# Loading batch 0's input in 96-row and 7-row pieces, and issuing the first tables and the mixing weights after the ninth unit's write

## The chip, the cores and the metric

One core of a Trainium2 chip runs the whole program. The metric is the device time of one execution in microseconds. An execution's span is the time from its first to its last instruction in the profile; the device time is a little more.

## What is computed

The reference has two parts: a spectral mixing layer over 8 sequences of 2496 rows of 256 numbers, and a mixture of experts over the 19968 rows that come out.

```python
X = np.fft.rfft(x, axis=1)                       # x: 8 x 2496 x 256
Yr = Xr @ w_r - Xi @ w_i + b_r
Yi = Xr @ w_i + Xi @ w_r + b_i
Yr = np.sign(Yr) * np.maximum(np.abs(Yr) - lam, 0.0)      # Yi the same
y = np.fft.irfft(Y, n=x.shape[1], axis=1)
...
logits = x @ w_gate                              # x: y as 19968 x 256
# greedy: pairs (row, expert) by falling logit, 2496 rows for each of 8 experts
h = np.maximum(x[mask] @ w1[e], 0.0)
out[mask] = h @ w2[e]
```

## The kernel before, in words

The Fourier transform of 2496 = 39 x 64 points goes in stages. For each batch, **stage 1** multiplies by a table that holds three copies of the 39-point transform side by side. Its input tile has 117 rows: 39 row positions for each of three column groups j, which start 22 columns apart. One of 11 units is two columns: one matmul with 512 free elements, a copy out of PSUM, and a write to the scratch tensor T (called T1 in the code, L1102). **Stage 2** reads T back, transposed by the way it is laid out, into the tile sh (six reads in batch 0, L1108), and multiplies by the 64-point table FG (L1121). ACT and DVE split each result into a high and a low part (xTh, xTl, L1130 to L1133). **Stage 3** multiplies by the mixing weights wt (L1140), DVE adds the bias (L1146), ACT and DVE apply the threshold (L1147, L1148). Stages 4 and 5 are the inverse transform (L1156, L1187). Stages 2 to 4 go in ten pairs p of table columns, two to a pair. The router and the experts follow in one program.

The order of the work is set by a planner (class Plan). Each piece of work is a task with an engine, an estimated duration, a position number and its dependences; the planner simulates the engines and emits, on each engine, the ready task that can start first, ties by position. So another estimate or dependence early in the program changes the fixed order in which each engine's queue is filled. Input loads of batch 0 have positions from -90 upwards.

What matters for the change:

- Batch 0's input is loaded by SP at L1060: for each chunk of 2 or 4 columns three loads of 39 rows, one for each j, 18 loads in all. The first chunk goes to a tile xt, the others into the tile that later is sh.
- Stage 1 of batch 0 is L1084; the units' results go round the tiles s1st, s4st, yst and s2c (L1099 on DVE, L1097 on ACT).
- Loads of constants are issued on POOL. Chunk 0 of the table cF (columns 0 to 4) waits for unit 0's copy through a one-element copy on POOL, a "gate" (L978); chunk 1 (columns 4 to 10) waits for unit 6's copy; the mixing weights w_r and w_i (L1015), the biases (L1010) and w_gate (L1019) wait for unit 10's copy (L1008). The rest (cG, cD, cF's chunks 2 and 3) waits for the first result of stage 2.
- L997 to L1000 turn FG's columns, in groups of four, into the inverse table; a group needs its chunk of cF. After stage 1, TensorE runs 40 matmuls on zeros (L1093, L1094).
- SP's loads and stores and ACT's load share eight completion semaphores, so the k-th of them waits until the (k-8)-th has landed.

Of the kernel before, what the change touches and what calls it, by code (L numbers as in the profile page):

```python
# [19 lines left out]
N1, N2 = 39, 64  # L20
B, S, D, E, F_ = 8, 2496, 256, 8, 1024
# [50 lines left out]
def const_arrays():  # L72
    D1, Fm, G, D5 = dft_consts()
    two = lambda m: np.ascontiguousarray(np.stack(split(m)))
    return dict(cD1=np.concatenate([two(D1), D1.astype(np.float32)[None]]), cF=Fm.astype(np.float32), cG=two(G[:, 0]), cD5=two(D5))
# [841 lines left out]
WU = 10  # L917
# [3 lines left out]
def phase_a(K, H, x, w_r, w_i, b_r, b_i, w_gate, cD1, cF, cG, cD5, YD, LG, NB=B):  # L921

    nc, plan = K.nc, K.plan
# [117 lines left out]
    def batch(b):  # L1041
# [6 lines left out]
        for c, (g0, n) in enumerate(CH):  # L1048
# [4 lines left out]
            xt.append(t)  # L1053
            for j in range(3):
# [6 lines left out]
                add_dma(pos1(g0 / 2) - 1.5 if b else -90 + c, em, 39 * m * 1024, [], [x0, t] if c and not b else [t], after=last_sh)  # L1061
        T1, sh, ev = K.dram("T1", [128, 20, 256]), sb("sh", [128, 20, 256]), []
        for u in range(NU):
# [5 lines left out]
            k_, M, gs_, n = *((117, 120) if u < 10 else (78, 80)), slice(0, 2), 512  # L1069
# [33 lines left out]
            if not b and u == 10: last_sh.append(d)  # L1103
        shq = []
# [394 lines left out]
```

## Time and profile before

| | |
|---|---|
| median of 3 runs | 1552.83 us (1551.01 to 1554.67) |
| the profiled execution's own time | 1552.06 us |
| its span | 1549.9 us |
| TensorE (PE) busy | 1516.3 us, 98% of the span |
| VectorE (DVE) / ScalarE (ACT) / GpSimd (POOL) busy | 1071.6 / 856.3 / 669.1 us |
| mean granted TensorE clock | 0.994 |
| moved by DMA | 208.23 MB |

The profile's page gives shares of the whole span. The view by stretch gives, for a piece of the span, each engine's busy time with the number of instructions, the granted TensorE clock as a share of full speed, the mean busy share of the 16 DMA engines and what they moved. The chain of waits follows the work that ended last backwards, step by step. The timeline lists instructions in order of time, with the idle time ahead of one and what ended it. q1 is the queue of SP's transfers, q0 that of POOL's.

### The profile page before, as it was taken

What the parts mean: (1) busy time and instruction counts of PE and PEld (TensorE: products, weight loads), DVE (VectorE), ACT (ScalarE), POOL (GpSimd) and SP (SyncE); (2) the same over time, 40 slices, a digit from 0 to 9 for tenths busy, and PEclk for the clock granted to TensorE, in tenths of its full rate; (3) what the DMA queues carried; (4) which work ended last, traced back from release to release, by engine and by line L of the source; (5) the groups of instructions that cost most, each with busy time, mean ns of one, the idle gap of its engine ahead of it and who ended that gap; (6) DMA issues with size and microseconds to landing.
All of it is one profiled execution on the core that took longest, in us unless ns stands there. A gap on an engine that the chain in (4) does not pass through costs nothing.

```text
span 1549.9 us, 31539 instructions
## 1 busy us (share of the span) xinstructions
PE 1516.3 (98%) x10927; PEld 1357.0 (88%) x10927; DVE 1071.6 (69%) x3524; ACT 856.3 (55%) x1870; POOL 669.1 (43%) x891
## 2 busy tenths in 40 slices
PE   7999999999899999999999999999999999999998
PEld 5999999999778877888788989889989889989998
DVE  3676767677975684889889889897777765552321
ACT  2768888787678887544535334344343443553332
POOL 2246566564545445343334434434335343343332
PEclk9999999999999999999999999999999999999999
DMA  9678777877668567433213122121211212311110
GB/s 272 192 245 258 220 250 217 249 233 243 217 179 262 178 192 214 143 129 129 86 45 100 47 69 69 50 93 54 70 59 59 89 57 69 114 56 45 43 48 29
DMA packets 144199, 208.23 MB, mean 134 GB/s; under 512 B 28751, under 2 KB 108575, under 8 KB 144030
## 3 DMA queue, kind: packets, MB, share of 16 engines
q1 hardware_dynamic: 127244, 162.30, 33.8%
q0 software_dynamic: 16656, 43.77, 9.0%
q8 instruction: 88, 1.44, 0.4%
q14 instruction: 81, 0.66, 0.1%
q10 hardware_dynamic: 130, 0.06, 0.0%
HBM read 121.31 MB, written 84.75 MB: 133 GB/s over the span
## 4 chain that ended last, share of the span: by engine, by line
PE 81%; DVE 6%; issue 4%; ACT 3%; DMA 3%; POOL 1%; SPq 0%; POOLq 0%; DVEq 0%; ACTq 0%
PE ps L665 25%; PE ps L639 19%; PE ps L1140 11%; PE p L639 6%; PE ps L1121 4%; PE ps L1156 3%; PE p L1077 2%; PE p L1187 2%; PE ps L624 2%; PE both L1210 2%; PE p L1191 1%; ACT ajunk L510 1%; PE ps L658 1%; PE ps L1228 1%; DVE junk L423 1%
## 5 line engine op out<-in xcount | busy, mean ns | idle before, releaser
L1140 PE MATMUL ps<-wt,xTh 128*128 128x256 f32 x1280 | 243.4, 288 | 2.2 <-DVE y L1148 1.1
L1140 PEld LDWEIGHTS ps<-wt,xTh 128*128 128x128 f32 x1280 | 198.6, 189 | 10.5 <-issue 5.8
L1140 PE MATMUL ps<-wt,xTl 128*128 128x256 f32 x640 | 178.8, 279 | 0.0
L678 POOL DMA_INDIRECT out_dram<-xTh,li x64 | 67.1, 1048 | 249.4 <-ACT xTh L674 212.7
L423 DVE SCALAR_TENSOR_TENSOR junk<-h_m,st,h_AG 128x156 bf16<-128x156 f32 (+1 forms) x472 | 161.2, 387 | 2.6
L956 POOL TENSOR_TENSOR zl<-y,zh 128x512 fp32r<-128x512 f32 x80 | 106.4, 1330 | 119.3 <-ACT zh L953 115.4
L1217 POOL TENSOR_TENSOR yTl<-yr,yTh 128x468 bf16<-128x468 f32 (+1 forms) x88 | 96.9, 1103 | 118.4 <-ACT yTh L1216 109.6
L1140 PEld LDWEIGHTS ps<-wt,xTl 128*128 128x128 f32 x640 | 120.4, 188 | 0.2 <-DVE xTl L1133 0.2
L1121 PE MATMUL ps<-FG,sh 128*128 128x128 f32 x640 | 97.9, 281 | 5.0 <-DMA sh<-T 4.6
L678 POOL DMA_INDIRECT out_dram<-xTl,li x64 | 65.7, 1026 | 85.5 <-ACT xTl L674 68.9
L665 PE MATMUL ps<-FG,yTh 128*128 128x256 f32 x441 | 102.1, 282 | 0.0
L1121 PEld LDWEIGHTS ps<-FG,sh 128*128 128x128 f32 x640 | 87.3, 194 | 13.6 <-DMA sh<-T 5.0
L674 ACT COPY xTl<-ps 128x256 f32<-128x256 f32 x80 | 29.9, 373 | 124.2 <-PE ps L665 100.2
L956 POOL TENSOR_TENSOR s2l<-s2c,s2h 120x512 fp32r<-120x512 f32 (+2 forms) x60 | 77.2, 1291 | 42.5 <-DVE s2h L953 31.0
L674 ACT COPY xTh<-ps 128x256 f32<-128x256 f32 x72 | 26.9, 374 | 110.2 <-PE ps L665 93.0
L665 PE MATMUL ps<-FG,y 128*128 128x256 f32 x414 | 86.8, 281 | 0.0
L956 DVE TENSOR_TENSOR xl<-xt,xh 117x512 fp32r<-117x512 f32 (+1 forms) x66 | 65.4, 992 | 25.1 <-ACT xh L953 23.8
L1131 DVE TENSOR_TENSOR xTl<-ps,xTh 128x512 fp32r<-128x512 f32 x80 | 54.8, 686 | 39.9 <-ACT xTh L1130 39.6
L665 PEld LDWEIGHTS ps<-FG,yTh 128*128 128x128 f32 x441 | 74.3, 188 | 0.9
L1215 DVE TENSOR_TENSOR yr<-both,yTh 128x468 f32<-128x468 f32 (+1 forms) x77 | 48.2, 625 | 35.5 <-ACT yTh L1214 32.7
L1148 DVE SCALAR_TENSOR_TENSOR y<-ps,y 128x512 f32<-128x512 f32 x80 | 55.1, 688 | 21.9 <-ACT y L1147 20.4
L665 PE MATMUL ps<-FG,s1st 128*128 128x256 f32 x329 | 69.5, 285 | 0.0
(755 smaller groups left out, 5094.6 us busy)
## 6 DMA issues: line engine op xcount, KB each, us to landing
xt<-in_moe_w_dram SPq DMA_DIRECT2D x64, 512.0 KB
T<-s4st SPq DMA_DIRECT2D x80, 256.0 KB
sh<-T SPq DMA_DIRECT2D x39, 512.0 KB
s2c<-T SPq DMA_DIRECT2D x80, 240.0 KB
YD<-yst SPq DMA_DIRECT2D x80, 234.0 KB
T<-s1st SPq DMA_DIRECT2D x73, 240.0 KB
xt<-in_x_dram SPq DMA_DIRECT2D x105, 156.0 KB
sh<-in_x_dram SPq DMA_DIRECT2D x14, 156.0 KB
```

The costliest lines, as they stand in the source:

```text
L423: v(cols + 59 + 1400 * K.extra, p, lambda k=k: V.scalar_tensor_tensor(junk[k % 2].t[:, 0:cols], H.m[:, 0:cols], c.t[:, k // ng:k // ng + 1 ...
L639: T.matmul(ps.t[:, 0:w], lhsT=W1.t[:, a, m, 128 * ft:128 * ft + 128], rhs=x_.t[:, 0:w], start=q + m == 0, stop=q + m == 3)
L665: T.matmul(ps.t[0:M], lhsT=a.t[:, 128 * q:128 * q + M], rhs=W2.t[:, w_, ft], start=k == 0, stop=k == 23)
L674: else: plan.add('A', .27, pos + 1, lambda: A.copy(o.t[0:M], ps.t[0:M]), [ps], [o])
L678: ins = P.indirect_dma_start(out=self.out, out_offset=bass.IndirectOffsetOnAxis(ap=oi.t[0:M, oo + t:oo + t + 1], axis=0), in_=o.t[0:M], in ...
L956: lambda: eng.tensor_tensor(lb[1](), src(), hb[1](), op=OP.subtract), [srcb, hb[0]], [lb[0]])
L1121: T.matmul(ps.t[:, i, 128 * dt:128 * dt + 128], lhsT=sh.t[:, k, 128 * dt:128 * dt + 128], rhs=Ft.t[:, k], start=True, stop=True)
L1131: plan.add('V', dve(512), pos, lambda th=th, tl=tl, src=src, apart=apart: apart(V.tensor_tensor(cols(tl, 64, 192), src(), cols(th, 64, 192 ...
L1140: T.matmul(ps3.t[:, i], lhsT=a.t[:, i, dt, o:o + 128], rhs=wt[c].t[:, w, dt], start=n == 0, stop=n == 11)
L1148: plan.add('V', dve(512), pos + 1.282, lambda y=y, ps3=ps3, t=t: V.scalar_tensor_tensor(y.t, ps3.t, 0.0, t.t, op0=OP.max, op1=OP.subtract) ...
L1215: plan.add('V', dve(2 * W), pos + 0.376, lambda yh=yh, yr=yr, psT=psT, W=W: V.tensor_tensor(yr.t[:, :, 0:W], psT.t[:, :, 0:W], yh.t[:, 0, ...
L1217: yq.append(plan.add('P', pool(2 * W), pos + 0.376, lambda yh=yh, yl=yl, yr=yr, W=W: P.tensor_tensor(yl.t[:, :, 0:W], yr.t[:, :, 0:W], yh. ...
```

## The change

- Batch 0's input tile gets another row order: rows 0 to 95 hold row position n = 0 to 31 with its three j side by side (row 3n + j), rows 96 to 116 hold the seven positions 32 to 38 for each j. The stage-1 table is stored with the same order of rows (`first`).
- For each chunk SP issues one load of 96 rows. For the first chunk it also issues three loads of 7 rows. For the other chunks POOL issues the 7-row loads as seven larger ones that span two or three chunks. SP's 18 loads become 9, and POOL gets 7.
- The three gates of chunk 0, chunk 1 and the weights are replaced by one: a one-element memset on POOL into the tile of the ninth unit (u = 8, tile s1st), which has to wait until that unit's write to T has landed. Chunk 0, then w_r and w_i, the biases, chunk 1 and w_gate are issued behind it.
- The last unit's matmul takes 117 rows where it took 78.

```diff
+    first = np.array([39 * j + n for n in range(NM) for j in range(3)] + [39 * j + n for j in range(3) for n in range(NM, N1)])
+    return dict(cD1=np.concatenate([two(D1), D1[first].astype(np.float32)[None]]), ...
...
-            g = gate((at(0), at(6), at(0, 0), at(0, 0))[q])
-            add_dma(-50 + q if q > 1 else -99 + q, lambda k0=k0, k1=k1: P.dma_start(Ft.t[:, k0:k1], cF[:, k0:k1, :]), 65e3 * (k1 - k0), [], [Ft, BF_[q]], 'P', after=g)
+            g = gate(at(0, 0)) if q > 1 else gates['w8']
+            add_dma(-50 + q if q > 1 else (-99, -96.5)[q], lambda k0=k0, k1=k1: P.dma_start(Ft.t[:, k0:k1], cF[:, k0:k1, :]), 65e3 * (k1 - k0), [], [Ft, BF_[q]], 'P', after=g)
...
     def load_weights(after):
-        b = gates['s1st', 0, WU]
-        first = [plan.add('P', 0.15, -99, lambda: P.tensor_copy(spacer[0:1, 0:1], b.t[0:1, 0, 0:1]), [b])]
+        b, d = gates['wr']
+        first = gates['w8'] = [plan.add('P', 0.15, -99.5, lambda: P.memset(b.t[0:1, 0, 0:1], 0.0), [], [], after=[d], uses=[b])]
...
+            if not b:
+
+                def rows(p, r0, nr, src0, ap, g0=g0, n=n, t=t):
+                    return lambda: nc.sync.dma_start(t.t[r0:r0 + nr, 0:n, :], bass.AP(tensor=x.tensor, offset=x.offset + (src0 + g0) * D, ap=ap + [[1, n * D]]))
+                add_dma(-90 + c, rows(0, 0, 3 * NM, 0, [[64 * D, NM], [22 * D, 3]]), 3 * NM * n * 1024, [], [x0, t] if c else [t])
+                if not c:
+                    for j in range(3): add_dma(-90 + c, rows(0, 3 * NM + 7 * j, 7, 64 * NM + 22 * j, [[64 * D, 7]]), 7 * n * 1024, [], [t])
+                continue
...
+        if not b:
+            for c0, c1 in ((1, 3), (3, 6)):
+                g0, g1 = CH[c0][0], sum(CH[c1 - 1])
+                for j in range(3):
+                    for a, z, jj in ((g0, min(g1, 20 if j == 2 else g1), j), (20, g1, 1)) if j == 2 and g1 > 20 else ((g0, g1, j),):
+                        def late(j=j, a=a, z=z, jj=jj):
+                            P.dma_start(x0.t[3 * NM + 7 * j:3 * NM + 7 * j + 7, a - 2:z - 2], bass.AP(tensor=x.tensor, offset=x.offset + (64 * NM + 22 * jj + a) * D, ap=[[64 * D, 7], [1, (z - a) * D]]))
+                        add_dma(-95 + c0, late, 7 * (z - a) * 1024, [], [x0] + xt[c0:c1], 'P')
...
-            k_, M, gs_, n = *((117, 120) if u < 10 else (78, 80)), slice(0, 2), 512
+            k_, M, gs_, n = *((117, 120) if u < 10 else (78 if b else 117, 80)), slice(0, 2), 512
...
+            if not b and u == 8: gates['wr'] = (st, d)
```

What is left out places the lines above in their functions and sets NM = 32.

**POOL, from its first work of the program on.** Before (spacer copies are the gates):

```order
masks.py:199 AFFINE_SELECT h_idn<-h_idn 128x128
L978 COPY spacer<-s1st_232 1x1
L981 DMA FG_238<-cF 128x512
L978 COPY spacer<-yst_274 1x1
L981 DMA FG_238<-cF 128x768
L1008 COPY spacer<-yst_338 1x1
L1015 DMA y_343<-in_w_r_dram 128x2x256
L1015 DMA y_345<-in_w_i_dram 128x2x256
L1010 DMA bt<-in_b_r_dram 64x256
L1019 DMA y_357<-in_moe_w_gate_dram 128x2x8
L1010 DMA bt<-in_b_i_dram 64x256
```

With the change (the memset of s1st is the new gate):

```order
L1078 DMA sh_165<-in_x_dram 7x2048 x3
L1078 DMA sh_165<-in_x_dram 7x3072 x2
L1078 DMA sh_165<-in_x_dram 7x2560
L1078 DMA sh_165<-in_x_dram 7x512
masks.py:197 MEMSET h_idn 128x128
masks.py:199 ISA
masks.py:199 AFFINE_SELECT h_idn<-h_idn 128x128
L1010 MEMSET s1st_282 1x1
L983 DMA FG_336<-cF 128x512
L1017 DMA y_338<-in_w_r_dram 128x2x256
L1017 DMA y_343<-in_w_i_dram 128x2x256
L1012 DMA bt<-in_b_r_dram 64x256
```

Seven loads of input rows now come first on POOL, chunk 0 of cF moved from the first gate to the same gate as the weights, and chunk 1 and the second bias went further back.

**DVE, from the first mixing weight split to the second bias addition.** Here xTl is the low part of stage 2's result for pairs 0, 1 and 2, y the result of the threshold, xl the low part of batch 1's input, bt the bias. Before:

```order
L1131 TENSOR_TENSOR xTl_401<-ps_384,xTh_395 128x4x128
L1133 TENSOR_TENSOR xTl_401<-xTh_395,ps_384 128x4x64
L1012 TENSOR_SCALAR bt<-bt 128x256
L1131 TENSOR_TENSOR xTl_428<-ps_392,xTh_404 128x4x128
L1133 TENSOR_TENSOR xTl_428<-xTh_404,ps_392 128x4x64
L1146 TENSOR_TENSOR ps_415<-ps_415,bt 128x512
L1148 SCALAR_TENSOR_TENSOR y_467<-ps_415,y_465 128x512
L1131 TENSOR_TENSOR xTl_487<-ps_447,xTh_483 128x4x128
L1133 TENSOR_TENSOR xTl_487<-xTh_483,ps_447 128x4x64
L1146 TENSOR_TENSOR ps_452<-ps_452,bt 128x512
```

With the change, from pair 2 on:

```order
L1150 TENSOR_TENSOR xTl_474<-ps_454,xTh_463 128x4x128
L1152 TENSOR_TENSOR xTl_474<-xTh_463,ps_454 128x4x64
L958 TENSOR_TENSOR xl_481<-xt_357,xh_476 117x512
L958 TENSOR_TENSOR xl_490<-xt_357,xh_479 117x512
L1014 TENSOR_SCALAR bt<-bt 128x256
L1150 TENSOR_TENSOR xTl_500<-ps_459,xTh_486 128x4x128
L1165 TENSOR_TENSOR ps_399<-ps_399,bt 128x512
L1165 TENSOR_TENSOR ps_428<-ps_428,bt 128x512
L1152 TENSOR_TENSOR xTl_500<-xTh_486,ps_459 128x4x64
L958 TENSOR_TENSOR xl_524<-xt_379,xh_517 117x512
L1167 SCALAR_TENSOR_TENSOR y_535<-ps_399,y_526 128x512
```

Pair 0's bias addition (ps_415 before, ps_399 now) moved from before pair 2's split to behind pair 3's first split and behind two splits of batch 1's input.

**TensorE, between the matmuls on zeros and the first of stage 3.** Before:

```order
L997 MATMUL ps_348<-yr_183,FG_238 128x128 x3
L997 MATMUL ps_352<-yr_183,FG_238 128x128 x4
L1121 MATMUL ps_384<-FG_238,sh_364 128x128 x4
L1121 MATMUL ps_392<-FG_238,sh_364 128x128 x4
L1140 MATMUL ps_415<-wt_367,xTh_395 128x256 x2
```

With the change:

```order
L999 MATMUL ps_349<-yr_243,FG_336 128x128 x3
L1140 MATMUL ps_364<-FG_336,sh_340 128x128 x4
L1140 MATMUL ps_372<-FG_336,sh_340 128x128 x4
L1159 MATMUL ps_399<-wt_359,xTh_375 128x256 x2
```

The turn of the second column group (four matmuls of L997, now L999) left this place. Further on, TensorE's order has all 48 stage-3 matmuls of pairs 0 and 1 (L1159), then stage 2 of pairs 2, 3 and 4 (12 of L1140), two stage-1 units of batch 1, a turn of four, stage 2 of pair 5, a unit, two turns of four, a unit, and the last turn of four. Before, stage 2 of pair 2 stood between the stage-3 matmuls of pairs 0 and 1. From about the 280th matmul on, TensorE's order is the same in both kernels up to the end.

## Rows read from the trace of the kernel before

**Rows 1.** The page: busy time, share of the span and instructions of each engine.

```profile
PE 1516.3 (98%) x10927; PEld 1357.0 (88%) x10927; DVE 1071.6 (69%) x3524; ACT 856.3 (55%) x1870; POOL 669.1 (43%) x891
```

**Rows 2.** The chain of waits, first 60 us: start us, us, what.

```profile
3.29 4.50 DMA sh<-in_x_dram
...
19.09 4.61 DMA T<-yst
...
23.92 3.57 DMA sh<-T
...
27.53 3.79 PE ps L1121 x16
...
46.31 0.89 PE ps L997 x8
47.20 0.69 PE p L1077 x3
47.90 1.37 PE ps L1140 x12
```

**Rows 3.** Timeline, TensorE in stage 1 and the first turn: start us, us, what, idle ahead.

```profile
4.60 1.53 PE L1084 MATMUL p<-xt,xh 117*120 117x512 f32 x2
7.18 1.95 PE L1084 MATMUL p<-sh,xh 117*120 117x512 f32 x4 [1.05 <-DMA sh<-in_x_dram]
9.44 3.92 PE L1084 MATMUL p<-sh,xh 117*120 117x512 f32 x8 [0.31 <-DMA sh<-in_x_dram]
14.52 3.82 PE L1084 MATMUL p<-sh,xh 117*120 117x512 f32 x8 [1.16 <-DMA sh<-in_x_dram]
...
21.43 1.72 PE L997 MATMUL ps<-yr,FG 128*128 128x128 f32 x14
```

**Rows 4.** Timeline, SP's queue: first input loads.

```profile
0.75 1.25 SPq L1060 DMA_DIRECT2D xt<-in_x_dram  x3
2.05 8.08 SPq L1060 DMA_DIRECT2D sh<-in_x_dram  x15
```

**Rows 5.** By stretch: busy us (instructions) of each engine, PEclk, DMA share, GB/s.

```profile
7.00:10.00 3.00, 2.51 (x6) 1.00 (x7) 0.69 (x1) 0.59 (x1) 0.78 (x2) 1.00 0.92 253
15.00:18.00 3.00, 3.00 (x8) 0.87 (x6) 0.69 (x1) 1.14 (x2) 0.29 (x1) 1.00 1.02 341
```

**Rows 6.** DMA by queue, 20 to 22 us, then 22.5 to 24.5 us: packets, MB, share.

```profile
q1 hardware_dynamic: 748, 0.72, 103.7%
q0 software_dynamic: 2, 0.00, 0.1%
...
q0 software_dynamic: 202, 0.58, 83.6%
q1 hardware_dynamic: 86, 0.08, 11.0%
```

**Rows 7.** Timeline, POOL's issues and the ACT work that waits for the weights.

```profile
19.69 0.72 POOL L1015 DMA_DIRECT2D y<-in_w_r_dram  x1 [0.32 <-issue]
...
24.53 0.62 ACT L953 CAST wt<-y 128x512 fp32r<-128x512 f32 x1 [0.74 <-DMA y<-in_w_r_dram]
```

**Rows 8.** Timeline, DVE, batch 0's splits and batch 1's.

```profile
37.88 0.69 DVE L1131 TENSOR_TENSOR xTl<-ps,xTh 128x512 fp32r<-128x512 f32 x1 [0.83 <-ACT xTh L1130]
38.49 0.41 DVE L1133 TENSOR_TENSOR xTl<-xTh,ps 128x256 fp32r<-128x256 f32 x1
```

**Rows 9.** By stretch, half microseconds where the granted clock falls or returns.

```profile
25.50:26.00 0.50, 0.00 (x0) 0.00 (x0) 0.37 (x1) 0.45 (x1) 0.00 (x0) 0.98 0.95 333
32.50:33.00 0.50, 0.50 (x5) 0.50 (x5) 0.49 (x2) 0.00 (x0) 0.50 (x1) 0.69 0.92 361
...
105.50:106.00 0.50, 0.25 (x3) 0.05 (x1) 0.23 (x1) 0.16 (x1) 0.00 (x0) 1.00 0.98 336
...
107.50:108.00 0.50, 0.35 (x3) 0.36 (x4) 0.00 (x0) 0.50 (x2) 0.50 (x1) 0.90 0.00 0
...
111.00:111.50 0.50, 0.50 (x3) 0.37 (x2) 0.48 (x1) 0.41 (x1) 0.00 (x0) 0.69 0.38 121
```

More of the change, by code (lines that the diff above doesn't have):

```diff
@@ L20 @@
 N1, N2 = 39, 64
+NM = 32
 B, S, D, E, F_ = 8, 2496, 256, 8, 1024
@@ L74, in const_arrays @@
     two = lambda m: np.ascontiguousarray(np.stack(split(m)))
-    return dict(cD1=np.concatenate([two(D1), D1.astype(np.float32)[None]]), cF=Fm.astype(np.float32), cG=two(G[:, 0]), cD5=two(D5))
+    first = np.array([39 * j + n for n in range(NM) for j in range(3)] + [39 * j + n for j in range(3) for n in range(NM, N1)])
+    return dict(cD1=np.concatenate([two(D1), D1[first].astype(np.float32)[None]]), cF=Fm.astype(np.float32), cG=two(G[:, 0]), cD5=two(D5))
 class Buf:
@@ L1014, in load_weights @@
             st = sb("y1", [128, 2, 256])
-            add_dma(-99, lambda st=st, w=w: nc.gpsimd.dma_start(st.t, w.rearrange("(t p) e -> p t e", p=128)), 262e3, [], [st], 'P', first)
+            add_dma(-98, lambda st=st, w=w: nc.gpsimd.dma_start(st.t, w.rearrange("(t p) e -> p t e", p=128)), 262e3, [], [st], 'P', first)
             split(-9.5, st, lambda st=st: st.t, (wt[i], lambda i=i: wt[i].t[:, 0]), (wt[i], lambda i=i: wt[i].t[:, 1]), 'A', 'V', 512, after)
```

## The prediction

> **What bounds the kernel now.** I read the page first: TensorE is busy 98% of the span [rows 1], so time can be won only where it stands idle or runs slowly, and work that it gets on top costs its full length. The chain of waits shows where that is at the start [rows 2]: up to 27.5 us the chain runs mostly over transfers (input loads, the last write to T, 4.61 us, the first read back, 3.57 us), and from 27.53 us on it runs over TensorE. I call the start of stage 2 T0; it is 27.53 us. What comes ahead of T0 is the place of this change. From about the 280th matmul on both kernels issue TensorE's work in the same order, so what T0 gains, less what the new order loses before they meet, should reach the end.
>
> The timeline shows stage 1 [rows 3]: eleven units, 0.98 us each once fed, with waits for loads of 1.05, 0.31 and 1.16 us, together 2.52 us; it ends at 14.52 + 3.82 = 18.34 us. SP needs until 10.13 us to issue its 18 loads [rows 4], because from the eighth on each waits for an earlier one. While these loads run, 253 GB/s are moved; while the writes run, 341 GB/s [rows 5]. The last write is issued at 19.09, 0.75 us after stage 1, and lands at 23.70 [rows 2]: 4.61 us, because earlier writes still stand in front of it, and from 20 to 22 us SP's queue q1 alone fills the engines while POOL's q0 moves nothing, though a weight load was issued at 19.69 [rows 6, 7]. The weights move from 22.5 us on [rows 6], and ACT gets w_r at 24.53 [rows 7].
>
> Last, the clock [rows 3, 9]: TensorE stands idle from 21.43 + 1.72 = 23.15 us, the granted clock falls to half at 26.0 and returns at about 32.8, 5.3 us after T0. So 5.3 us of the path after T0 run at half speed.
>
> **The change, part by part.** Times are made against the profiled execution, 1552.06 us; the median of the runs shown is 0.77 us above it.
>
> *Loads in 9 instead of 18 pieces on SP.* Four loads stand ahead of unit 0 where three did, at 1.25 / 3 = 0.42 us each [rows 4], so unit 0 starts near 4.9 instead of 4.60 and ends near 6.4 (1.53 us) [rows 3]. SP has issued everything by about 0.75 + 9 x 0.42 = 4.5 us. Unit 1 also needs POOL's first three loads. POOL's issues cost 0.72 us for large loads [rows 7], so these three are out by about 2.9; how long a small load on q0 takes this early, no row shows. The bounds are 2.6 us (unit 0's load: issued by 2.00, used at 4.60 [rows 3, 4]) and 4.1 us (w_r: issued by 20.41, used at 24.53 in a full queue [rows 7]): 5.5 to 7.0, and I take 6.6 for unit 1, against 7.18. At the old rate, 253 GB/s, all 2.6 MB (2496 rows of 1 KB) are in by 12.3 us, counted from 2.0, when the first three loads are issued; at 341 GB/s, by 9.6. TensorE needs the last chunk only at 6.6 + 8 x 0.98 = 14.4, so ten units run through, 9.8 us, and stage 1 ends at 16.4: 1.9 us earlier. With unit 1 at 7.18 it would be 1.5 (all but the first wait), with no wait at all 2.5.
>
> [...]
>
> *Chunks 0 and 1 and the weights behind the ninth write.* Before, 0.65 MB of cF went between the loads and writes, and the weights competed with the last writes. Now q1 has only loads and writes up to the gate. At 341 GB/s the 2.6 MB of writes need 7.6 us after the loads, so by bytes they end between 17.2 and 19.9; the last is issued at 16.4 + 0.75 = 17.15. Its landing takes between 2.6 us (the load above) and 4.61 us (as before); with little in front of it I take the low end: 19.75 instead of 23.70, 3.95 us earlier.
>
> The gate itself: unit 8's write is issued near 15.2 and lands near 17.7; then POOL issues chunk 0, w_r and w_i at 0.72 us each [rows 7], by 19.9, and the first bias and chunk 1 by 21.2. At 4.1 us from issue to use, chunk 0 is there at 22.6 and w_i at 24.0. Stage 2 needs chunk 0; stage 3 needs w_r only after stage 2 of two pairs, 3.79 us after T0 [rows 2]. So neither blocks, but 1.2 MB of them now move together with the first reads of T. Read alone, the first takes 3.57 us [rows 2]; the 0.45 MB that still move then would add up to 1.3 us at 341 GB/s. I take 0.7: T0 = 19.75 + 0.25 + 3.57 + 0.7 = 24.25, **3.3 us earlier**. With the worse ends (stage 1 only 1.5 us earlier, 4.61 us for the last write, 1.3 us of sharing) T0 is 27.3, 0.2 us earlier; with the better ones (2.5, 2.6 and 0) it is 23.0, 4.5 us earlier.
>
> *Turning the second column group.* It ran in idle time ahead of T0 (its chunk came early); now it runs between other work: four matmuls, for which the chain has 0.89 us (x8, as each of these matmuls is two passes; the seven of before T0 stand as x14 [rows 3]) [rows 2]: **+0.9 us**.
>
> *The new order after T0.* Stage 3 of pairs 0 and 1 now runs in one piece: from T0 + 3.8, four times 1.4 us [rows 2], and 0.75 more for the part at half speed, to T0 + 10.1. Then stage 2 of pairs 2, 3 and 4 stands in a row, 0.9 us each (half of the 1.8 us for eight at full clock, by the 0.89 us of four), but there are two PSUM tiles for it: pair 4 waits until ACT and DVE have taken pair 2, 0.6 [rows 7] + 0.6 + 0.3 us [rows 8] after its end with gaps of 0.1, so about T0 + 12.8 where TensorE arrives at 11.9: 0.9 us. Pair 5 waits for pair 3's last split, and DVE has two splits of input, the bias, a split, two bias additions ahead of it, 0.6 us each: T0 + 16.6, where TensorE arrives at about 16.0 after two units (0.69 each [rows 2]) and a turn: 0.6 us. Together **+1.5 us**; bounds 0 (DVE gains enough, as it idles while TensorE does stage 3) and 2.5 (each DVE piece 0.69 instead of 0.6). The second bias, now behind the gate on xTh and cG, lands by about T0 + 9 and is needed at T0 + 13.9: nothing.
>
> *The clock.* TensorE's idle time ahead of T0 shrinks: the matmuls on zeros end at 16.4 + 3.3 = 19.7, the first turn runs for 0.7 us once chunk 0 is in, and then it waits for T. So one idle piece of 4.4 us becomes two of 1 to 3 us. In the trace a piece of 1.16 us had no effect [rows 3], and one of 1.9 us, 105.75 to 107.65, did: the clock fell at 107.9 and was back at 111.2, 3.6 us after work began again [rows 9]. I take it that the clock falls again and returns as it did there: 1.7 us less at half speed, **-0.8 us**. Bounds: 0, and -1.9 if it does not fall (stage 3 must then wait for the splits, or it would be -2.6).
>
> *Nothing:* 117 instead of 78 rows in the last unit (the same 512 columns); the identity behind POOL's loads, done by about 6.5 us and needed by DVE at 7; the table's new row order (made on the host).
>
> Sum: -3.3 + 0.9 + 1.5 - 0.8 = **-1.7 us**, 1550.4 us.
>
> **Rivals.**
>
> *The clock stays up.* For it: two short idle pieces instead of a long one. Against it: rows 9 show a fall after 1.9 us. Then -3.3 + 0.9 + 1.5 - 1.9 = -2.8: 1549.3 us.
>
> *The new order costs nothing.* DVE stands idle while TensorE does the long piece of stage 3; both waits are under 1 us and rest on gaps of 0.1 us between instructions that I only assumed. Then -1.7 - 1.5 = -3.2, with the clock up -4.3: 1548.9 to 1547.8 us.
>
> *POOL's rows come late: slower.* From 20 to 22 us q0 moved nothing while q1 had a backlog [rows 6]. If q0 gets its turn only when q1 is drained, unit 1 waits for SP's 2.2 MB, to about 10.5 us at 253 GB/s, instead of 6.6. Everything after it shifts by 3.9 us: -1.7 + 3.9 = +2.2, 1554.3 us. The point from which the change is slower is unit 1 starting at 8.3 us. Against it: the same rows fit a start-up of some 2 us. [...]
>
> *It doesn't do what it says.* The writes end where they ended, since bytes and not order bind: T0 as before, only the costs remain, +2.4 with the clock as it was: 1554.5 us. Against it: the loads' 253 GB/s beside 341 [rows 5] and 2.5 us of waits in stage 1.
>
> **How the numbers follow.** Chances: forecast 0.36, clock stays up 0.28, order free 0.20, late rows 0.11, nothing gained 0.05. A measurement of this kernel tells about 0.2% from no change, 3.1 us: below 1549.0 or above 1555.2. The forecast (T0 can be 1.2 us better and 3.1 worse) is below 1549.0 in a fifth of cases, the second case in four of ten, the third in four of five: 0.07 + 0.11 + 0.16 = 0.34, to which the low ends of T0 in the rest add 0.04: faster 0.38. Slower: the upper part of the last two, 0.07. The rest, 0.55, is within 0.2%. The range runs from the third case with the clock up and T0's better bound, 1547.8 - 1.2 = 1546.6, to the late rows and the nothing gained, 1554.4; the forecast's own range is 1549.2 to 1553.5.
>
> **What would show it.** Right: unit 1 at 6 to 7 us and no wait inside stage 1 later; its end near 16.4; the last write's landing near 19.8; q0 empty from 12 to 18 us; T0 near 24.2; TensorE waiting for DVE before pairs 4 and 5. Wrong: stage 1 waiting on POOL's loads; T0 later than 26; stage 3 waiting for the weights; a clock that stays full through T0; or a stall near 105 us that grows or goes with the new phase of batch 1's loads.

## The result and the profile after

The change makes the kernel **slower by 0.53%**: ratio 1.0053 to the kernel before on the same chip, 95% interval 1.0043 to 1.0063 (medians 1560.1 and 1554.27 us, nine runs each). On another chip, beside other runs, it was 1.0049 (1.0033 to 1.0065). Forecast were 1550.4 us and no loss; the slowest case that the prediction priced was 2.4 us above the kernel before, and measured are 5.8.

The profiled execution took 1564.1 us, the longest of the nine; its span is 1561.8, 11.9 more than the 1549.9 of the profile before. So its parts below add up to twice the difference of the medians. The page, to [rows 1]: TensorE has 4 us more of work and 12 us more of span.

```profile
PE 1520.4 (97%) x10927; PEld 1358.8 (87%) x10927; DVE 1070.7 (69%) x3524; ACT 856.7 (55%) x1870; POOL 670.6 (43%) x896
```

The timeline of TensorE shows where the 12 us begin. These rows answer to [rows 3]; L1102 is stage 1, L999 the turn, L1140 stage 2, L1095 batch 1's first unit.

```profile
7.59 1.44 PE L1102 MATMUL p<-xt,xh 117*120 117x512 f32 x2 [2.79 <-DMA xt<-in_x_dram]
12.95 12.06 PE L1102 MATMUL p<-sh,xh 117*120 117x512 f32 x20 [3.92 <-DMA sh<-in_x_dram]
24.95 2.18 PE L1111 MATMUL ps<-xh 64*128 64x256 f32 x32
...
30.36 0.94 PE L999 MATMUL ps<-yr,FG 128*128 128x128 f32 x6 [2.10 <-DMA FG<-cF]
...
32.42 2.08 PE L1140 MATMUL ps<-FG,sh 128*128 128x128 f32 x8 [1.12 <-DMA sh<-T]
35.34 2.08 PE L1140 MATMUL ps<-FG,sh 128*128 128x128 f32 x8 [0.85 <-DMA sh<-T]
...
46.52 1.13 PE L1140 MATMUL ps<-FG,sh 128*128 128x128 f32 x8 [0.93 <-PE ps L1140]
49.14 0.73 PE L1095 MATMUL p<-xh,d 117*120 117x512 f32 x1 [1.49 <-DMA d<-cD]
```

Unit 0 starts at 7.59 instead of 4.60, unit 1 at 12.95 instead of 7.18. From there ten units run without a wait, in 12.06 us because the clock is low at first (below), but T0 comes at 32.42 instead of 27.53: **4.9 us later**. Then TensorE waits again, last for cD, the table of batch 1's first stage. The chain of waits answers to [rows 2]:

```profile
2.75 10.07 DMA sh<-in_x_dram
...
25.77 2.44 DMA T<-yst
...
28.48 3.89 DMA sh<-T
...
37.16 11.85 DMA d<-cD
```

By stretch, the clock (third number from the right) answers to [rows 9]. It fell at 8.20, behind the wait of 2.79 us ahead of unit 0, again at 32.10 in the idle time ahead of T0, and a third time at 49.16, at the end of the wait for cD (1.49 us), each time to 0.50:

```profile
8.00:12.00 4.00, 1.03 (x2) 0.00 (x0) 1.11 (x6) 0.00 (x0) 0.00 (x0) 0.53 1.04 145
12.00:16.00 4.00, 3.05 (x4) 1.39 (x5) 0.00 (x0) 0.59 (x1) 0.00 (x0) 0.50 1.00 208
...
34.00:36.00 2.00, 1.15 (x6) 0.86 (x5) 0.85 (x2) 1.44 (x3) 0.63 (x4) 0.50 0.95 336
...
50.00:52.00 2.00, 2.00 (x6) 1.48 (x5) 0.92 (x3) 1.10 (x2) 0.00 (x0) 0.50 0.60 188
```

Where the two orders have met again, the same matmul (the 329th record of TensorE) starts at 60.98 before and at 72.57 now: 11.6 us, all but 0.3 of this execution's loss. Of it 4.9 lie ahead of T0 and 6.7 behind: 3.27 of waits (0.85, 0.93, 1.49), 0.9 of the moved turn, 1.9 of clock (5.7 us of work at half speed behind T0 and 3.4 at the third fall cost 4.5, against 2.6 before); 0.6 us remain that no row names.

So there are two questions: why the loads came late, and why more was lost behind T0.

### The profile page after: what moved, and what is told of

Same layout as the page of the kernel before. It is cut to its first block, busy times and chain, and to the rows that moved or that the text cites. A ratio compares the mean times of both kernels' runs of the same rounds, so it can differ in the third digit from the quotient of the medians.

```text
span 1561.8 us, 31539 instructions
## 1 busy us (share of the span) xinstructions
PE 1520.4 (97%) x10927; PEld 1358.8 (87%) x10927; DVE 1070.7 (69%) x3524; ACT 856.7 (55%) x1870; POOL 670.6 (43%) x896
## 4 chain that ended last, share of the span: by engine, by line
PE 81%; DVE 6%; DMA 4%; ACT 3%; issue 3%; POOL 1%; SPq 0%; POOLq 0%; DVEq 0%; ACTq 0%
PE ps L667 25%; PE ps L641 19%; PE ps L1159 10%; PE p L641 6%; PE ps L1140 4%; PE ps L1175 3%; PE p L1095 3%; PE p L1206 2%; PE ps L626 2%; PE both L1229 2%; PE p L1210 1%; ACT ajunk L512 1%; PE ps L660 1%; PE ps L1247 1%; DMA T<-s1st 1%
## 5 line engine op out<-in xcount | busy, mean ns | idle before, releaser
L1159 PE MATMUL ps<-wt,xTh 128*128 128x256 f32 x1280 | 243.6, 288 | 2.2 <-DVE y L1167 1.1
L1159 PEld LDWEIGHTS ps<-wt,xTh 128*128 128x128 f32 x1280 | 198.9, 189 | 10.3 <-issue 5.9
L1159 PE MATMUL ps<-wt,xTl 128*128 128x256 f32 x640 | 179.0, 280 | 0.3 <-DVE xTl L1152 0.3
L1159 PEld LDWEIGHTS ps<-wt,xTl 128*128 128x128 f32 x640 | 120.5, 188 | 0.5 <-DVE xTl L1152 0.5
L1140 PE MATMUL ps<-FG,sh 128*128 128x128 f32 x640 | 98.5, 283 | 3.4 <-DMA sh<-T 2.0
L1140 PEld LDWEIGHTS ps<-FG,sh 128*128 128x128 f32 x640 | 87.6, 195 | 12.4 <-issue 4.1
L667 PE MATMUL ps<-FG,yst 128*128 128x256 f32 x314 | 69.5, 283 | 0.0
```

What stands on the lines that cost most here:

```text
L667: T.matmul(ps.t[0:M], lhsT=a.t[:, 128 * q:128 * q + M], rhs=W2.t[:, w_, ft], start=k == 0, stop=k == 23)
L1140: T.matmul(ps.t[:, i, 128 * dt:128 * dt + 128], lhsT=sh.t[:, k, 128 * dt:128 * dt + 128], rhs=Ft.t[:, k], start=True, stop=True)
L1159: T.matmul(ps3.t[:, i], lhsT=a.t[:, i, dt, o:o + 128], rhs=wt[c].t[:, w, dt], start=n == 0, stop=n == 11)
```

## The experiments

All are timed against the kernel before on the same chip; the chips differ from group to group. "Wait" is the longest wait of TensorE for a transfer, or for what waits for one, between T0 and 60 us; times of unit 1 and T0 are from each one's profile.

| run | loads | gate | unit 1 | T0 | wait | ratio (95%) |
|---|---|---|---|---|---|---|
| the change | new | new | 12.95 | 32.42 | 1.49 | 1.0053 (1.0043 to 1.0063) |
| after_again | new | new | 10.83 | 29.57 | 4.00 | 1.0049 (1.0033 to 1.0065) |
| before_again | old | old | 7.18 | 28.16 | 0.33 | 0.9992 (0.9976 to 1.0008) |
| loads_only | new | old | 10.52 | 33.86 | 0.77 | 1.0027 (1.0017 to 1.0037) |
| gate_only | old | new | 7.34 | 28.17 | 4.20 | 1.0042 (1.0027 to 1.0056) |
| gate_cd | old | new, cD early | 6.79 | 26.99 | 5.57 | 1.0051 (1.0037 to 1.0065) |
| gate_u5 | old | at unit 5 | 6.87 | 28.95 | under 0.4 | 1.0016 (1.0007 to 1.0025) |
| rows117 | one of 117 rows | new | 7.91 | 27.96 | 2.41 | 1.0025 (1.0012 to 1.0037) |
| no_tail | 96 rows alone | new | 6.30 | 22.35 | 3.53 | 1.0007 (0.9997 to 1.0017) |
| no_tail_old | 96 rows alone | old | 6.06 | 24.36 | under 0.4 | 0.9989 (0.9976 to 1.0002) |
| tail21_old | 96 + 21 rows | old | 9.26 | 29.71 | 2.20 | 1.0004 (0.9993 to 1.0016) |
| tail21_old_cd | 96 + 21 rows | old, cD early | 8.17 | 27.87 | 1.35 | 1.0010 (0.9998 to 1.0022) |
| tail21_cd | 96 + 21 rows | new, cD early | 8.55 | 25.41 | 5.46 | 1.0039 (1.0025 to 1.0053) |
| tail4k_old | late rows cut to 4 KB | old | 7.68 | 32.99 | under 0.5 | 1.0028 (1.0016 to 1.0041) |
| before_warm | old | old, more matmuls on zeros | 7.07 | 27.94 | 1.43 | 1.0015 (1.0004 to 1.0027) |

### Which half of the change costs

**loads_only** takes the gates and their positions back to the lines of before:

```diff
-            g = gate(at(0, 0)) if q > 1 else gates['w8']
+            g = gate((at(0), at(6), at(0, 0), at(0, 0))[q])
...
-        first = gates['w8'] = [plan.add('P', 0.15, -99.5, lambda: P.memset(b.t[0:1, 0, 0:1], 0.0), [], [], after=[d], uses=[b])]
+        first = [plan.add('P', 0.15, -99, lambda: P.tensor_copy(spacer[0:1, 0:1], b.t[0:1, 0, 0:1]), [b])]
```

Expected: 

> The new loads with the gates and the weights' place of before; all other engines have the order of before. Unit 1 late as with the change (11 to 13 us), T0 near 32 us, 4 to 5 us later than before. Theory 1 (late loads are the whole loss): about as slow as the change, 1559 to 1562. Theory 2 (gate has its own loss): offset against before stays at what it is at T0, so 1557 to 1559.5, less than the change by 2 us or more in the profiled execution.

**gate_only** is the kernel before with the same lines the other way round.

Expected: 

> The loads of before (18 pieces of 39 rows), with only the new gate for the first tables and the weights. All theories: unit 0 at 4.6 us and stage 1 ending near 18.3 as before. Theory 1 (everything lost comes from the late loads, and the wait for cD and the second fall of the clock come only from the delay): T0 a little earlier than before (26 to 27.5 us) and the time within 2 us of before, 1552 to 1556. Theory 2 (the gate has a loss of its own: the turn of the second column group inside busy time, 0.9 us, waits for PSUM and for cD, 1 to 2.5 us): T0 as early, but the offset grows by 2 to 5 us between T0 and 60 us, time 1555 to 1559.

Each half alone is slower, by 0.27% and 0.42%; together that is more than the 0.5% of both, so the two losses overlap. loads_only bears out that late loads are not the whole loss: its profile is 6.3 us behind at T0, 7.6 at 60 us (a wait of 0.77 us for cG) and 6.1 at 150 us, so next to nothing is lost behind T0. In the median it lost 4.0 us, less than either theory said. gate_only refutes that the loss behind T0 only came from late loads: its profile is 0.6 us behind at T0 and 8.4 at 60 us, more growth than the 2 to 5 us of its second theory. With loads in time TensorE waits for chunk 0 and for cD (timeline, TensorE), and ACT for batch 1's input (timeline, ACT), which it split at 38.26 before.

```profile
26.73 1.65 PE L997 MATMUL ps<-yr,FG 128*128 128x128 f32 x6 [4.72 <-DMA FG<-cF]
...
44.94 0.75 PE L1077 MATMUL p<-xh,d 117*120 117x512 f32 x1 [4.20 <-DMA d<-cD]
```

```profile
42.31 1.14 ACT L953 CAST xh<-xt 117x512 fp32r<-117x512 f32 x2 [9.23 <-DMA xt<-in_x_dram]
```

**after_again** and **before_again** are the two kernels unchanged.

Expected: 

> The change once more, beside the others of this call. Theory: unit 1 at 10 to 13.5 us, with nine shares of the first large load landing together and seven 2 us or more later; T0 over 29; a wait of ACT for batch 1's input or of TensorE for cD after T0; 0.4 to 0.6% slower than before. If the first profile was chance, unit 1 before 9 us and T0 under 28.

Expected: 

> The kernel before once more, for a second profile: how far stage 1's waits for loads, T0, the clock ahead of it and the stall near 105 us repeat themselves. If they are a matter of the kernel: waits in stage 1 of 2 to 3 us in sum, T0 at 27 to 28.5, half speed for some 5 us behind it, the stall of 1.9 us at 106 with a fall of the clock. If they are chance, one or more of these is missing.

The pattern repeats: late unit 1, T0 1.4 us after that of before_again, a wait for cD (4.00 us). Its parts don't: 2.1 us lie between the two profiles' unit 1, and before_again has its stall at 106 us without a fall of the clock; in the first profile of the kernel before that fall cost 1.4 us.

### The loads: seven engines

**no_tail** drops all 7-row loads and sets stage 1's rows to 96, so 21 of the 117 rows of each product are left out; **rows117** sets NM = 39 and drops them too, but loads every row.

Expected: 

> The change without any 7-row load; batch 0's stage 1 multiplies only the 96 rows that the large loads bring, so 21 of the 117 rows of each stage-1 product of batch 0 are left out. The order on the engines is that of the change. Theory A (the 7-row loads hold up seven engines): the 16 shares of a large load land together, 4 KB packets take about 230 ns, unit 1 at 6 to 7 us, stage 1 ends at 16 to 17.5, T0 at 24 to 26. Theory B (the 96-row order on 16 engines is read slowly by itself): 4 KB packets take 350 ns or more and 2 MB come at 150 to 200 GB/s, so units wait one after another and stage 1 ends after 18.

Expected: 

> The change with all 117 rows of a chunk in one SP load, row 3n + j for all n = 0 to 38, and no 7-row load at all: 6 loads in place of 9 and 7. Theory A (the 7-row loads sit on seven DMA engines and hold up the shares of the large loads there): unit 0 near 4.5 us, unit 1 at 6 to 7.2, stage 1 without a wait over 1 us and ending at 16 to 17.5, T0 at 24 to 26, packets of 4 KB taking about 230 ns, and a time of 1550 to 1556. Theory B (the order with three j side by side is itself read slowly): packets of 4 KB still take 350 ns or more, stage 1 waits again and ends after 19, T0 after 27.5, time 1556 or more.

no_tail does what the prediction wanted of the loads: no wait at all in stage 1, its end at 15.99, T0 at 22.35. Its TensorE timeline:

```profile
6.30 9.69 PE L1092 MATMUL p<-sh,xh 96*120 96x512 f32 x20
...
21.58 0.94 PE L999 MATMUL ps<-yr,FG 128*128 128x128 f32 x6 [2.34 <-DMA FG<-cF]
...
27.25 0.39 PE L1149 MATMUL ps<-wt,xTh 128*128 128x256 f32 x1 [1.35 <-ACT wt L955]
...
40.44 0.65 PE L1085 MATMUL p<-xh,d 117*120 117x512 f32 x1 [3.53 <-DMA d<-cD]
```

So the 96-row order is not read slowly. rows117 shows that it isn't only the bytes left out: with every row and no 7-row load a 4 KB packet takes 217 ns and unit 1 starts at 7.91. That is still a wait of 1.84 us, stage 1 ends at 18.97 and T0 stays at 27.96, behind a wait of 4.30 us for chunk 0, so its forecast of an earlier T0 failed. The 7-row loads are the cause of the late loads. DMA by queue from 4 to 12 us (packets, MB, share), of the change and then of no_tail:

```profile
DMA packets 386, 1.15 MB, mean 144 GB/s; under 512 B 137, under 2 KB 137, under 8 KB 364
q1 hardware_dynamic: 264, 0.92, 81.7%
q0 software_dynamic: 122, 0.24, 18.3%
```

```profile
DMA packets 999, 2.24 MB, mean 280 GB/s; under 512 B 102, under 2 KB 570, under 8 KB 999
q1 hardware_dynamic: 999, 2.24, 101.5%
```

The engines are full in both, and half as much arrives. A 4 KB packet of q1 took 433 ns between 4 and 8 us, 217 before and 244 in no_tail (means of the trace's packet records). The size of this effect varies: the second profiles have 345 ns and 182 GB/s for the change, 272 ns and 200 GB/s for the kernel before. How the first large load's 16 shares landed (us, semaphore events of the traces) shows the place:

```
the change   7.76 7.78 7.82 7.88 7.92 7.95 7.98 8.00 8.72 | 10.68 10.79 10.80 10.86 11.18 11.38 12.81
after_again  7.16 7.21 7.29 7.38 7.46 7.47 7.58 7.59 7.79 | 8.45 8.58 8.63 10.04 10.06 10.42 10.69
no_tail      4.80 4.99 5.05 5.18 5.22 5.26 5.28 5.29 5.34 5.42 5.44 5.45 5.50 5.62 5.68 5.69
```

Nine shares together, seven late. POOL's 7-row loads land the same way: of the first one's 16 shares nine come between 3.46 and 3.90 and seven between 5.11 and 5.65. In the records such a load is seven packets, one a row, of 8 to 12 KB in six of the seven loads; in the first profile they start seven at a time (3.54 to 3.65, 3.94 to 4.14, 5.07 to 5.35, 7.10 to 7.45), and in both profiles of the change never more than seven packets of 8 KB or more run at a time, though several such loads are under way. No record names a packet's engine. I read from these counts that each long row is on one engine, that one load after another uses the same seven, and that these seven also carry the late shares of the large loads (the next one landed nine by 10.88 and seven from 15.21 on). POOL's own loads for unit 1 had landed by 8.18; what TensorE waited for was the seven late shares of SP's load, the last at 12.81.

Four runs ask why long rows on seven engines slow all 16 (the nine early shares of the change's first three large loads are in by 8.72, 10.88 and 13.26, so 2.2 to 2.4 us for a load of 0.39 MB that no_tail's 280 GB/s would bring in 1.4). Each was executed once, as was the kernel before beside them (1558.15 us), so their times say little; what counts are the packets. tail_sp issues the late rows on SP behind the chunks that they belong to, tail_4k cuts them by chunk (17 loads instead of 7), tail_spread puts them on every third partition and also joins the first chunk's three 7-row loads into one, tail_pitch reads them 65 rows apart. The lines shown are the main ones.

```diff
tail_sp
-                            P.dma_start(x0.t[3 * NM + 7 * j:
+                            nc.sync.dma_start(x0.t[3 * NM + 7 * j:
tail_4k
-            for c0, c1 in ((1, 3), (3, 6)):
+            for c0, c1 in ((1, 2), (2, 3), (3, 4), (4, 5), (5, 6)):
tail_spread
-                            P.dma_start(x0.t[3 * NM + 7 * j:3 * NM + 7 * j + 7, a - 2:z - 2]
+                            P.dma_start(x0.t[3 * NM + j:3 * N1:3, a - 2:z - 2]
tail_pitch
-ap=[[64 * D, 7], [1, (z - a) * D]]
+ap=[[65 * D, 7], [1, (z - a) * D]]
```

Expected: 

> The change with the seven late 7-row loads issued by SP behind the chunks that they belong to, instead of by POOL; the same rows, sizes and targets, so queue q0 moves nothing in stage 1. Theory A1 (two queues on the same engines slow each other): without q0 the packets of 4 KB take about 250 ns as without the 7-row loads, and unit 1 starts at 7 to 8.5 us. Theory A2 (the 7-row loads are slow in themselves, whatever the queue, since 7 engines carry rows of 8 to 12 KB): packets of 4 KB over 350 ns, 110 to 200 GB/s between 4 and 12 us, unit 1 after 10 us.

Expected: 

> The change with the late 7-row loads cut by chunk: rows of 4 KB in 17 loads instead of 8 to 12 KB in 7, still on POOL. Theory A3 (the long rows are what holds up the other packets): packets of 4 KB of q1 fall from 430 to about 250 ns, unit 1 at 7 to 9 us, no later wait for SP's loads. Rival (length doesn't matter): 430 ns as before, unit 1 after 11 us, and POOL's issues, 17 of 0.55 us, make the last chunks later still.

Expected: 

> The change with the 7-row loads going to every third partition (row 96 + 3i + j) instead of 7 partitions side by side, and the first chunk's three 7-row loads as one of 21 rows. Theory A4 (seven engines write to neighbouring partitions and share their way in): the 8 KB packets of q0 fall from 0.85 to 1.1 us towards the 0.31 us of the first seven, 4 KB packets of q1 from 430 to about 250 ns, unit 1 at 7 to 9 us. Rival (the place in the target doesn't matter): as with the change, unit 1 after 11 us.

Expected: 

> The change with the late 7-row loads reading rows 65 instead of 64 sequence positions apart (65 KB instead of 64 KB), so that stage 1 gets wrong rows there. Theory A5 (the memory is slow for rows a power of two apart that are read at the same time): 4 KB packets fall from 430 ns to under 300 and unit 1 starts before 9 us. Rival (the distance doesn't matter): as with the change, 4 KB packets at about 430 ns and unit 1 at 11 to 14 us.

| run | time us | unit 0 | unit 1 | 4 to 12 us, GB/s | 4 KB packet of q1, 4 to 8 us |
|---|---|---|---|---|---|
| the kernel before; again | | 4.60; 4.60 | 7.18; 7.18 | 237; 200 | 217; 272 ns |
| the change; again; loads_only | | 7.59; 7.15; 7.33 | 12.95; 10.83; 10.52 | 144; 182; 182 | 433; 345; 361 ns |
| tail_sp | 1572.06 | 4.60 | 9.80 | 212 | 273 ns |
| tail_4k | 1564.06 | 5.56 | 7.62 | 252 | 252 ns |
| tail_spread | 1566.18 | 6.46 | 8.28 | 241 | 251 ns |
| tail_pitch | 1569.41 | 7.06 | 10.32 | 196 | 313 ns |

Shorter rows and spread targets both mend most of it (4 to 12 us, tail_4k, then tail_spread):

```profile
DMA packets 746, 2.02 MB, mean 252 GB/s; under 512 B 247, under 2 KB 256, under 8 KB 746
```

```profile
DMA packets 604, 1.93 MB, mean 241 GB/s; under 512 B 171, under 2 KB 171, under 8 KB 575
```

tail_sp lies between its two theories. TensorE's timeline:

```profile
4.60 1.34 PE L1102 MATMUL p<-xt,xh 117*120 117x512 f32 x2
9.80 6.49 PE L1102 MATMUL p<-sh,xh 117*120 117x512 f32 x8 [3.87 <-DMA sh<-in_x_dram]
```

Without POOL's rows unit 0 is in time, the first large load has landed whole by 7.43, and the 4 KB packets are nearly as fast as in the kernel before. But the long rows are slow on SP too, 1148 ns for 12 KB (880 and 1112 in the two profiles of the change), and it is they that hold unit 1 to 9.80. So the queue does not make them slow; but running on q0 early and beside SP's loads they held up unit 0 and the first large load. Whether it is the queue or the time that counts there, tail_sp does not separate. The distance between rows shows no effect beyond what two profiles of the same loads differ by. That rows of 8 to 12 KB into neighbouring partitions are the trouble is what tail_4k and tail_spread point to: their packets lie outside the three profiles with these loads unchanged (345 to 433 ns) and within the two of the kernel before. It rests on one profile each, and the mechanism is not shown: no record tells of a way in that neighbouring partitions share, as theory A4 has it.

### The gate: empty engines, then too many bytes

**gate_cd** is gate_only with cD behind unit 0's copy (`g = gate(at(0))`, position -98.9). **gate_u5** is gate_only with `u == 5` in place of `u == 8`.

Expected: 

> Only the new gate with the old loads, as in the run before, and cD issued behind unit 0's copy (near 7 us) instead of behind stage 2's first result. Theory G1 (the gate's loss is mostly the wait for cD, 4.20 us, and the slow clock behind it): no wait of batch 1's first unit for cD, the clock stays at full speed from 40 to 50 us, the offset against the kernel before falls from 8.4 to 2 to 4 us at 60 us, and the time by 4 to 6 us, to within 2 us of before. Theory G2 (chunk 0 of cF, which ended the wait ahead of T0, and the weights are the loss): cD no longer waits, but another transfer is waited for in its place, since the same bytes come after T0, and the time falls by under 2 us.

Expected: 

> Only the new gate with the old loads, but hung on unit 5's write instead of unit 8's. Theory D (with the gate at unit 8 the DMA engines run half empty from 22 to 26 us, while POOL and TensorE wait for the landing, and the 1.2 MB of tables and weights then push batch 1's input and cD back): POOL's tables go out at 17 to 19.5 us as the weights did before, no stretch from 20 to 26 us under 280 GB/s, batch 1's input is split by ACT at 37 to 40 us instead of 42.3, no wait over 2 us before batch 1's first unit, and the time is 3 to 6 us below the gate at unit 8: 1551 to 1555. Rival (bytes sharing with stage 1's writes is what costs, so earlier is no better): T0 later than 28.5 and the time no lower than with the gate at unit 8, 1556 to 1560.

gate_cd gains nothing: TensorE's wait of 4.20 for cD becomes 5.57 for ACT's split, since batch 1's input now lands at 44.7. So not one transfer is late but all of them. By stretch, before, gate_only and gate_u5:

```profile
20.00:26.00 6.00, 3.15 (x30) 2.83 (x27) 1.94 (x3) 2.32 (x4) 2.94 (x5) 1.00 0.93 311
26.00:32.00 6.00, 4.47 (x21) 4.47 (x22) 2.94 (x10) 1.61 (x4) 1.51 (x5) 0.50 0.95 349
32.00:38.00 6.00, 6.00 (x50) 6.00 (x50) 2.51 (x5) 1.82 (x4) 1.62 (x3) 0.93 1.12 250
38.00:44.00 6.00, 6.00 (x49) 5.70 (x49) 5.19 (x10) 5.88 (x13) 1.28 (x1) 1.00 0.85 210
```

```profile
20.00:26.00 6.00, 2.01 (x24) 1.67 (x20) 0.00 (x0) 0.00 (x0) 2.99 (x6) 0.85 0.63 192
26.00:32.00 6.00, 5.27 (x28) 5.27 (x28) 2.22 (x4) 2.47 (x5) 2.26 (x6) 0.58 1.04 377
32.00:38.00 6.00, 4.76 (x38) 4.36 (x38) 2.53 (x8) 1.05 (x3) 2.59 (x5) 1.00 1.09 325
38.00:44.00 6.00, 2.75 (x25) 2.55 (x23) 1.04 (x2) 1.69 (x4) 0.00 (x0) 1.00 1.03 216
```

```profile
20.00:26.00 6.00, 2.19 (x11) 1.69 (x9) 0.98 (x2) 1.51 (x3) 4.12 (x7) 0.70 0.90 275
```

Behind the gate the engines are 0.63 busy where they were 0.93, and move 192 instead of 311 GB/s for 6 us: 0.71 MB less. The gate's chain in gate_only is unit 8's write, 17.65 to 22.40, the memset, chunk 0 issued at 23.09 and in use at 26.73:

```profile
17.65 4.75 DMA T<-s1st
...
23.09 3.59 DMA FG<-cF
```

What the weights did before in that hole comes later, on top of the reads of T and batch 1's input, and the engines are then full until 44 us (shares over 1). Hung on unit 5 the hole is gone (275 GB/s), no wait of 0.4 us or more follows T0, and 0.42% becomes 0.16%. T0 is later, 28.95 (28.16 in before_again), as the rival said; that the tables now share with stage 1's writes is its reason and is not shown apart.

### What a mended version is worth

**no_tail_old** is no_tail with the old gates; **tail21_old** (the old gates), **tail21_old_cd** and **tail21_cd** load a chunk's 21 rows at once, in rows of at most 4 KB:

```diff
+                    P.dma_start(t.t[3 * NM:3 * N1, 0:n], bass.AP(tensor=x.tensor, offset=x.offset + (64 * NM + g0) * D, ap=[[64 * D, 7], [22 * D, 3], [1, n * D]]))
```

Expected: 

> The 96-row loads without any 7-row load (21 of 117 rows of each stage-1 product of batch 0 left out) and with the gates and order of before. Theory D: the loads' gain is real and the gate alone ate it: stage 1 ends at 16 to 17, T0 at 23 to 24.5 us, 3 to 4.5 earlier than before, the order is that of before, batch 1's input comes in time, and the time is 2 to 4.5 us below before, 1547 to 1550. Rival (the first 45 us are bound by bytes, so that an early T0 only waits later for cG, cD or batch 1's input): T0 as early, but waits for DMA of 2 us or more before 50 us and a time within 1.5 us of before.

Expected: 

> [...] Theory A4 or A3 (rows of 8 to 12 KB into neighbouring partitions were the trouble): 4 KB packets about 250 ns, unit 0 near 5 us, unit 1 at 6.3 to 8 us, stage 1 ends at 16.5 to 18.5, T0 at 25 to 27.5. With T0 about 1 us earlier than before and the order of before: 1550 to 1554. [...]

Expected: 

> The same with cD issued behind unit 0's copy. If cD is not waited for in the run without this (as in the kernel before), nothing is gained: within 1 us of it. If T0 comes so early there that cD is waited for, up to 4 us faster than it.

Expected: 

> The change with the mended loads (21 rows in one load per chunk) and cD behind unit 0's copy, the other tables and the weights behind the new gate. If the two causes are the whole loss (7-row loads, cD), then stage 1 runs as in the run without 7-row loads, T0 at 23 to 25.5 us, no wait for cD, and the time is 1546 to 1551. If the gate itself (chunk 0 of cF issued only when unit 8's write has landed) costs, TensorE waits for cF ahead of T0 by over 1.5 us and the time is no better than with the old gates.

**tail4k_old** is tail_4k with the old gates.

Expected: 

> The new loads with the late rows cut to 4 KB and the gates of before: the mended loads and the old gates together, a candidate for a faster kernel. Theory (rows of 8 to 12 KB spoil the loads, the gate spoils what follows): 4 KB packets of q1 about 250 ns, unit 1 at 6.5 to 8 us, T0 at 25 to 28, no wait after T0 over 2 us, and the time within 0.15% of before on either side (0.2% faster at best, 0.2% slower if POOL's 17 issues hold up the last chunks).

no_tail_old starts stage 2 3.2 us earlier than before, with no wait of note behind it:

```profile
24.36 3.79 PE L1129 MATMUL ps<-FG,sh 128*128 128x128 f32 x16 [3.85 <-DMA sh<-T]
```

The same matmuls are 2.9 us earlier at 200 us, 1.6 at 800 and 0.7 at 1200. That drift is no larger than the one between the two profiles of the kernel before, so the gain is seen early and not shown at the end. Timed, no_tail_old is 0.11% faster, with an interval that holds no change (0.9976 to 1.0002); the kernel before, unchanged, came out at 0.9992. And it leaves out 18% of the rows. With the same loads and the new gate no_tail gives 1.0007: 0.18%, or some 2.8 us, more. All versions that load every row lose that gain again: with 21 rows in one load unit 1 comes at 8.17 to 9.26 us (7.18 before; no faster than before), and in tail4k_old POOL waits for unit 0's copy with ten of its 17 late loads still behind it in its order; the first of them, issued at 7.88, takes 7.56 us to land, and unit 5 waits 2.78 us. No version here beats the kernel before.

### The clock's price

**before_warm** lengthens the matmuls on zeros ahead of T0:

```diff
-                            for i in range(WARM): T.matmul(psw[0].t, lhsT=zr.t[:, 0:128], rhs=zr.t, start=i == 0, stop=i == WARM - 1)
+                            for i in range(34): T.matmul(psw[0].t, lhsT=zr.t[:, 0:128], rhs=zr.t, start=i == 0, stop=i == 33)
```

Expected: 

> The kernel before with 34 instead of 8 of the long matmuls on zeros after stage 1 (26 more of about 0.15 us, 3.9 us), so that TensorE has no long idle time ahead of T0; no other instruction differs. It measures the clock's part: the matmuls on zeros end near 25.3, the first turn near 27.1, T0 stays at 27.3 to 27.8 and the granted clock stays at full speed from 26 to 33 us. Half of the 5.3 us that ran at half speed after T0 is then won: 2.6 us, 1548.5 to 1550, if batch 1's input and cD come in time for it; 0 to 1 us if TensorE then waits for them.

The clock stays at 1.00 through T0, and the first 16 stage-2 records take 2.05 us instead of 3.79 [rows 2]. It wins nothing: TensorE then waits for DVE and for cG, at 60 us it is where before_again is to 0.1 us, and 1.0015 is slower, if anything.

```profile
27.94 2.05 PE L1121 MATMUL ps<-FG,sh 128*128 128x128 f32 x16 [1.03 <-DMA sh<-T]
30.92 0.38 PE L1140 MATMUL ps<-wt,xTl 128*128 128x256 f32 x1 [0.64 <-DVE xTl L1131]
...
40.71 0.35 PE L1156 MATMUL ps<-zh,FG 128*128 128x256 f32 x1 [1.43 <-DMA FG<-cG]
```

## Why the prediction was wrong

Two steps failed: how fast the loads come, and what the bytes moved behind T0 hold up.

- **Unit 1 at 6.6 us, ten units run through, stage 1 ends at 16.4.** This step failed. I bounded when POOL's first loads land and took the old rate for the rest. POOL's loads did land by 8.2, but the old rate did not hold (144 and 182 GB/s between 4 and 12 us, where the kernel before moved 237 and 200), because I took a load's bytes as spread over all engines. Measured: unit 0 at 7.59 and 7.15 where I had 4.9, unit 1 at 12.95 and 10.83, the end at 25.0 and 22.7. SP was done with issuing at 6.0, not 4.5. Without the 7-row loads the step is right: 6.30, no wait, 15.99.
- **The late-rows rival** had the right side and the wrong mechanism: q0 moved 0.24 MB beside q1's 0.92 between 4 and 12 us, and POOL's loads for unit 1 had landed by 8.18; what came late were shares of SP's own loads (seven of the first large one's, 10.68 to 12.81).
- **The last write's landing, 2.6 us.** Right: 2.44 (25.77 to 28.21), where it was 4.61.
- **"Neither blocks": chunk 0 by 22.6, w_i by 24.0.** Right only as far as stage 1 is in time: in no_tail chunk 0 is used at 21.58, but the weights cost 1.35 + 0.34 us. With the old loads unit 8's write takes 4.75 us to land, not 2.5, and chunk 0 sets T0.
- **What else hangs on the bytes moved behind T0.** Not in the sum, and the largest omission: I checked chunk 0, the weights and the second bias, not batch 1's input on SP's queue and cD on POOL's. Behind a late gate they cost 1.5 to 5.6 us of wait, and gate_only's 0.42% is their price, chunk 0's and the moved turn's together.
- **The turn, +0.9, and pair 4's wait, 0.9.** Right: 0.93 in the row above. Pair 5's 0.6 us does not appear; the wait for cD stands in its place.
- **The clock, -0.8.** Wrong in sign for the change as it ran: the clock fell twice more, at 8.20 behind a wait of 2.79 us and at 49.16 behind one of 1.49. In no_tail, where the loads came in time, the clock stayed at 1.00 to 40.56, through T0, so there the rival "the clock stays up" came true. before_warm shows that full speed behind T0 was worth nothing while transfers set the pace. The comparison it rested on is weak as well: the stall at 106 us let the clock fall in the kernel before, and not in before_again (and by [rows 9] it was back at 111.3, not 111.2).
- **The gain of an early T0** is seen in the profile when the gates stay: 3.2 us at T0 and 2.9 at 200 us in no_tail_old; the times do not show it. That the sum gave -3.3 for T0 is chance: no_tail_old has another gate and fewer rows, and with the predicted gate no_tail reached T0 5.2 us earlier and was still no faster.

## What to carry to other kernels

Count a load's engines, not its bytes, and look at how the shares of one load land: here, with a few long rows beside it, a wide load had nine shares in by 8.72 us and the last of the other seven at 12.81, and cutting or spreading the long rows brought unit 1 from 12.95 to 7.62 and 8.28 (though no version beat the kernel before). Before transfers are moved behind an event, ask what the engines do until then (here 0.63 busy where they were 0.93), and add the bytes up to the next consumer of every queue, not only of the moved ones. A slow TensorE cost nothing here while transfers set the pace (before_warm, with the clock at 1.00 through T0, is at 60 us where before_again is, to 0.1 us): take such a term only where the next wait is not a DMA.

## What was not expected of the hardware

Seven loads of 14 to 84 KB on queue q0 cut what 16 full engines moved to 144 and 182 GB/s in the change's two profiles, against 280 without them, and cutting or spreading them brought it back to 252 and 241. The same 1.9 us stall near 106 us ended with a fall of the granted clock in one profile of the same kernel and with 1.00 throughout in another; the stretch below is of before_again and answers to the last three of [rows 9].

```profile
107.00:108.00 1.00, 0.00 (x0) 0.00 (x0) 0.82 (x2) 0.48 (x1) 0.00 (x0) 1.00 0.57 186
...
110.00:111.00 1.00, 1.00 (x8) 0.91 (x8) 1.00 (x3) 0.79 (x2) 0.74 (x1) 1.00 0.33 107
```

cD, 0.11 MB in rows of 480 bytes, took 11.9 to 14.1 us from issue to landing while the engines were full (8.3 in the kernel before).
